# Chunk 0's inverse in two separate chains by halves of the heads, its first MLP layer split by token halves, and a new order of all steps

## The chip, the cores and the metric

The kernel runs on one core of a Trainium2 chip. The metric is the device time of one execution in microseconds (us), lower is better. Five engines work side by side: TensorE (PE, matrix products, with PEld for its weight loads), VectorE (DVE), ScalarE (ACT), GpSimd (POOL) and SyncE (SP, which here only issues loads and stores). ACT and POOL issue some loads too.

## The reference

Four batch rows of 768 tokens with eight heads of 48 columns pass through a delta rule (a matrix state per head, corrected token by token), and the result through one normalised MLP with 1536 hidden columns and a residual.

```python
k_n = k / (norm(k) + 1e-06)
for t in range(S):
    y[:, :, t] = einsum('bhd,bhde->bhe', q[:, :, t], state)
    v_old = einsum('bhde,bhd->bhe', state, kt)
    state = state + bt * einsum('bhd,bhe->bhde', kt, vt - v_old)
x = y.transpose(0, 2, 1, 3).reshape(B, S, H * D)          # (4, 768, 384)
xn = (x - mu) / sqrt(var + 1e-06) * g_ln
out = x + maximum(xn @ w_ch1, 0) @ w_ch2                   # 384 -> 1536 -> 384
```

## The kernel before

**Chunks.** The 768 tokens are worked in 12 chunks of 64. With two batch pairs and the heads there are 32 small problems per chunk; they lie in two halves, g = 0 and g = 1 (eight heads each of two batch rows). Inside a chunk the delta rule is a triangular system: with G = K K^T (`gram`) one needs an inverse X of a unit triangular matrix, then u = X v (`prod_u`), the output y (`out_y`), and the new state (`state_up`). After that come the layer norm (`xln`), its transpose with the factor g_ln (`xnt`), and the MLP of the chunk (`mlp`). Chunk 1's inverse, and those of the pairs 2-3, 4-5 and so on, are made row by row on DVE (`rows_inverse`, lines 916 and 923: two small operations a row).

**Chunk 0's inverse** (`first_inverse`, lines 716 to 802) is on the way of everything at the start, and so is made by doubling. After a first block (multiply L752, predicated copy L761, transposes L767, and three ACT copies `back`, L738) there are five levels n = 1..5. A level of a half g is: product E (PE, L780, 16 products of 64 by 64), a predicated copy out of PSUM (DVE, L785), product Z (PE, L795), and two ways out of Z's PSUM tile: two DVE transposes (`nat`, L744, needed by E of the next level) and three ACT copies (`back`, L738, needed by Z of the next level). Which PSUM pair a product writes comes from a list `order` (L1599): the pairs `two`, `by` and `f0/f1` in turn, i % 3. A product may only overwrite a pair when all readers of what was there are done. A pair `f0/f1` is two tiles, so that its predicated copy is two operations; the others need one.

**Chunk 0's u, y, norm.** u of half g goes to `two` (g = 0) or `by` (g = 1), L1078; y L1104; x L1142 on ACT; statistics on DVE; xln L1160; the transposes of both halves to `by` (L1192); xnt L1208 on ACT for g = 0 and L1198 on DVE for g = 1.

**MLP of chunk 0** (`mlp(0)`, L1409). The first layer is 12 blocks of 128 hidden columns, each three products (L1416) of 128 rows by 256 tokens, both halves at once, then one relu on ACT (L1425). fp32 products show up twice in the trace, so a block is six matmul rows. The second layer (L1438) is two sums of 12 products.

**Order.** Nothing is scheduled on the chip. The steps are recorded with `add`, each with its engine and what it reads and writes, and the list `ORDER` (L131) says in which order they are emitted; `in_this_order` keeps that order on each engine. An `f` in the list is a product of zeros (`zeros`, L1591, two matmul rows) that gives PE something to do. In the built program each load or store on the queues of SP and ACT also waits for the one eight places earlier in that written order (both queues counted together) to have landed. SP's loads of the diagonal blocks `gb` for chunk 1's inverse (from `gd`, the stored gram matrix) are in that chain, and ACT's square root `nrm_b` (L892) reads them.

**Weights.** The MLP weights come as 64-bit words and are converted on chip: two ACT operations (`hi` L593, `lo` L601), one DVE shift (L598) and one POOL sum (L611) for each piece. These fill the first 75 us beside chunk 0.

**End.** The last chunk's results go out by `put` (L1455): four stores on SP.

Of the kernel before, what the change touches and what calls it, by code (L numbers as in the profile page):

```python
# [16 lines left out]
C = 64  # L17
# [114 lines left out]
53 9 54 8 47 0 10 76 52 1 11-12 5 13 57 35 39 4 79 55 48 59 61 36 58 49 66 37 80 56 38 43 62 40 75 6-7 65 71 86 257  # L132
89 63 85 96 90 41 91 24 18 97 42 81 44 98 2 23 64 73 26 99 15 21 92 87 82 69 83-84 14 88 33 100 50 402 105 101-102
74 93 104 94 30 95 72 17 106 20 19 124 107 103 108 118 70 109 16 125 77 110 226 119 111 27 29 32 31 112 126 128 120
f f f 133 127 123 130 325 121-122 67 78 129 404 238 113 215 326 114 131 134 406 115-116 132 22 234 f 135 117 316 216
141 136 34 137 147 144 140 209 403 145 138 411 142 139 143 146 407 148-149 214 222 68 151 150 228 210 264 240 157
265 211 154 262 155 25 153 232 315 28 227 156 212 266 229 162 313 152 248 159 f 163 414 158 230 165 164 260 160-161
314 166 51 168 244 167 263 174 170 259 220 169 261 239 173 180 176 241 327 171 175 172 181 409 45 177 183 246 217
245 410 182 178 184 328 179 250 258 413 f f 185 60 191 189 256 317 242 401 186-187 196 46 193 190 197 192 188 247
318 194 199 267 195 213 198 268 319 363 200-201 243 269 205 320 270-271 273 203 f 321 272 208 274 202 275-276 204  # L140
277 249 207 278 322 251 279-280 3 364 281 f f 329 282 206 283 224 284 638 337 285-286 323 339 287 331 324 330 340
288 332 650 342 289-290 370 338 333 469 344 291-292 235-236 341 293-294 369 295-296 334 297 347 335 298-300 252 223
336 348 301 405 231 302 343 225 408 218 f f f f f 361 303 237 304 352 254 353 412 345 640 362 253 652 346 354 477
415 f 435 349 233 365 350 359 475 434 255 219 351 367 309 366 308 360 437 368 f f 355 310 376 375 312 436 221 358 f
f f 438 311 399 356-357 306 382 575 416 307 439 642 305 470 577 641 474 576 473 476 579 578 639 371 417 440 373 381
581 372 377 767 374 580 614 379 378 583 418 387 380 442 419 584 388 766 478 587 479 420 480-481 582 482 485 585 769
588 394 484 400 486 421 487 586 488-489 393 654 490-491 385 615 492 637 771 493 422 383 591 768 644 494 764 651 495
389 423 589 649 496 592 497-498 424 499 590 656 500 772 501 643 502 770 503 763 595 504 428 505 426 773 506 395 507
593 390 425 508 427 596 509 429 510 441 511 433 512 431 645 432 616 430 397 599 513 1052 443 514 594 396 655 391 515
653 444 516 483 517 398 774 600 445 518 1054 908 601 907 446 448 447 519 1056 910 520 909 521 657 522 646 449 384  # L150
523 386 629 451 597 524 647 1055 525 452 392 526 450 648 527 453 1051 454 528 658 1064 1058 617 659 602 1066 598 660
603 455 912 765 458 456 529 618 459 530 619 531 1053 532 620 533 1057 621 534-535 604 661 665 605 536 460 662 606
537-538 663 607 630 608 539 457 609 540-541 664 610 542-544 775 545 631 546 461 547 776 465 548 622 902 467 466 611
623 913 462-463 900 624 464 468 625 666-667 778 668-670 550 626 672 777 1068 673 911 549 805 674-675 551 676-678 809
632 806 679 552 680 807 681 1158 682-683 633 613 811 808 1157 684 810 685 914 686 813 687 904 688-689 1159 690 815
1059 814 627 812 901 817 691 1526 905 553 1160 692 554 693 818 694 816 819 695 556 779 555 557-558 823 696 1528 820
697-698 559 471 824 699 821 829 560 832 700 562 915 830 561 1070 563 822 780 701 1063 1163 702 831 564 838 906 781
703 825 704-705 1530 706 839 784 707 1067 1164 634 1165 708 782 612 785 835 709 786 565 710 1525 787 840 836 711 841
788-789 842 791 833 843 1167 792 472 712 827 783 628 834 1156 713 916 671 714 1166 828 844 715 1162 826 793 855 569
903 716 848 567 837 717 849 1155 568 790 718 850 1069 566 856 719 794 1168 857 720 858 845 721 1169 859 722 851 1529  # L160
795 723 852-853 796 847 860 724 917 797 846 570 862 801 725 571 918 726 1532 798 727 802 728 1531 854 800 865 729
799 1527 866 730 804 873 731 803 732 1065 874 573 733 875 734 574 919 735 920 736 572 921 1170 867 922 861 1352 876
635 877 1344 878 636 923 739 1071 868 740 956 924 869 957 737 870 1060 871 879 738 872 880 1537 1061 925 1161 1062
1072 948 891 1073 892 881 949 882 927 1074 883 926 1345 884 930 885 864 931 962 1354 953 1538 741 863 1171 886 951
742 1079 1172 958 887 1077 980 928 888 1346 929 893 752 1075 932 894 1076 935 895 963 746 1350 1173 1078 959 744 743
896 1540 964 897 950 936 1175 960 1533 965 954 745 1174 961 983 937 933 955 939 747 966 984 934 749 952 981 751 750
982 938 748 968 1080 940 967 1081 1356 1082 985 1348 1176 1083 969 1084 1087 1347 974 889 1177 1086 1351 1088-1090
1355 972 1091 975 1092 890 1093-1094 942 1095 989 1096 970 898 1097-1098 1634 1099-1100 1178 1353 971 1203 1101 973
944 1102 1180 1103 1824 2014 1104-1105 1630 753 1542 1106 1179 990 1358 1204 756 991 941 978 1085 1357 1107 899 986
992 979 1349 976 1108 987 943 1109 996 993 1633 977 999 1110 754 1000 997 1111 757 994 1001 755 1112 2016 1002 995  # L170
1359 1016 988 1017-1018 947 998 1003 1637 945 1006 2013 1007 946 1008 1205 1004 1019 1005 1020-1021 1113 1009 1639
1022 1024 1114 1010 1636 1023 1011 1031 1014 1115 1360 1012 1116 1209 1117 758 1641 1118 1025 1119 1640 760 1541
1026 1120 759 1629 1032 1361 1013 761 1027-1028 1218 1029 1211 1033 1030 1642 1362 1222 1182 1643 1207 1181 1185
1638 1042 1183 1631 1034 1015 1186 1035 1190 1043 762 1121 1036 1208 1122 1212 1184 1123 1213 1187 1124 1044 1544
1214 1045 1125 1046 1364 1543 1047 1363 1226 1126 2018 1037 1188 1048 1365 1038 1191 1049 1192 1189 1215 1366 1127
1219 1128 1216 1129 1367 1130 1230 1193 2017 1220 1131-1132 1223 1221 1368 1231 1224 1539 1227 1217 1534 1039 1225
1206 1194 1232 1535 1195 1228 1133 1632 1245 1233 1229 1239 1050 1259 1234 1240 1264 1536 1235 1545 1246 1241 1236
1254 1247 1134 1248 2026 1135 1196 1250 1249 1136 1210 1546 1644 1041 1242 1137 1547 1829 1138 1251 1197 1139 1243
1252 1040 1260 1244 1261 1198 1265 1140 1262 1199 1255-1256 1237 1548 1263 1266 1828 1141 1253 1257 1369 1142 1258
1143 1267 1645 1144 1268 1145 1269 1146 1201 1147 1273 1646 1270 1238 1274 1282 1276 1283 1271 1275 1284-1285 1280  # L180
1148 1286 1272 1149 1551 1292 2028 1287 1150 1658 1277 1288 1552 1202 1278 1550 1200 1290 1299 1293 1279 1294 1300
1289 1301 1831 1302 1281 1295-1296 1303 1635 1309 1553 1310 1297 1152 1304 1549 1298 1311 1305 1312 1317 1291 1396
1833 1318 1307 1830 1319 1554 1313 1151 1392 1314 2030 1320 1153 1315 1321 1308 1324 1322 1154 1306 1325 1323 1393
1834 1555 1371 1399 1326 1556 1335 1316 1397 1825 1557 1370 1336 1558 1561 1337 1823 1394 1327 1821 1395 1328 1560
1407 1329 1832 1562 1338 1403 1330 1339 2015 1372 1408 1373 1331 1340 1398 1400 1411 1563 1401 1341 2031 1564 1343
1409 1374 1402 1412 1404 1647 1826 1410 2032 1405 1565 1835 1413 1566 1406 1426 1414 1567 1648 1568 1440 1415 1427
1423 1649 1569 1420 1376 1445 1651 1377 2029 1421 1375 1570 1650 1416 1435 1422 1424 1332 1652 1417 1379 1334 1653
1380 1571-1572 1428 1381 1654 1660 1431 1657 1655 1429 1656 1378 1432 1430 1659 1382 1418 1433 1661 1425 1446 1573
1662 1574 1441 1836 1447 1419 1436 1434 1437 1448 1663 1575 1449 1383 1438 1450 1384 1333 1442 1576 1439 1577 1451
# [68 lines left out]
def kernel(  # L258
# [131 lines left out]
    def half(e):  # L390
        return slice(C * e, C * e + C)
# [638 lines left out]
    def recur(c, pr, lag=0.0):  # L1030
# [158 lines left out]
        for g in range(2) if c <= LNPE else ():  # L1189
            def turn(g=g):  # L1190
                for t in range(KC):
                    nc.tensor.transpose(by[:, g, t * 128 : (t + 1) * 128], xlns[g][:, t * 128 : (t + 1) * 128], ident)  # L1192
# [259 lines left out]
    def o_keys(g):  # L1452
        return [("o", g, n) for n in range(2)]
# [285 lines left out]
```

## Time and profile before

| what | value |
|---|---|
| runs | 534.24, 537.71, 536.07 us; median 536.07 |
| the profiled execution | 533.75 us, of which the profile's span is 532.0 |
| PE busy | 497.6 us (94%) |
| DVE, POOL, ACT busy | 366.4, 281.3, 207.9 us |
| first E product / last Z product of chunk 0's inverse | 21.70 / 46.58 us |
| chunk 0's first MLP product | 68.32 us |
| product of chunk 1's queries (`two` <- `qt,kt`, L828) | 67.23 us |
| last product ends / the four last stores are issued / span ends | 527.24 / 526.93 to 529.49 / 532.0 us |

A profile row such as "L785 DVE COPY_PREDICATED gsb<-u,two 128x512" is line 785 of the kernel, on DVE, writing `gsb` from `u` and `two`. Behind a bar stand the busy time and the mean time of one; behind a second bar the idle time of that engine just before, with what ended it. "issue" means that the engine waited for nothing that the profile shows.

### The profile page before, as it was taken

To read this page: it belongs to the slowest core of one execution; us is meant where nothing else is said; L and a number is where in the kernel's file an instruction comes from. 1 tells how busy PE (TensorE), PEld (TensorE's weight loads), DVE (VectorE), ACT (ScalarE), POOL (GpSimd) and SP (SyncE) were. 2 spreads that over 40 slices of the span, in tenths; PEclk is the share of its full clock that TensorE was granted. 3 is DMA by queue.
4 is the path that set the end of the run, shared out by engine and by line. 5 is a ranking of instruction groups with operands and counts; after the bars stand their busy time and mean duration, and the time that the engine had idled before them with its cause. 6 is when DMAs were issued, how large, how long until landed. Compare 5 with 4: busy or idle time off the path is not lost.

```text
span 532.0 us, 22724 instructions
## 1 busy us (share of the span) xinstructions
PE 497.6 (94%) x9942; PEld 451.9 (85%) x9942; DVE 366.4 (69%) x819; ACT 207.9 (39%) x451; POOL 281.3 (53%) x447
## 2 busy tenths in 40 slices
PE   5978798989989999999999999999999999999996
PEld 2766676758778888899999899999999999999996
DVE  3677748899996697994799982789985546244241
ACT  5677645412423332343342433442422623524130
POOL 6015574460573948757827617464266353554554
PEclk9789999999989999999999999999999999999999
DMA  9948798357635657156625157532435411212011
GB/s 174 289 73 194 178 207 160 78 111 139 119 58 120 150 115 123 34 141 154 100 65 97 21 135 198 116 70 33 101 74 104 91 31 37 56 40 53 1 30 31
DMA packets 181635, 54.56 MB, mean 103 GB/s; under 512 B 164888, under 2 KB 177312, under 8 KB 181536
## 3 DMA queue, kind: packets, MB, share of 16 engines
q1 hardware_dynamic: 168672, 40.30, 37.2%
q10 hardware_dynamic: 10656, 9.64, 6.6%
q0 software_dynamic: 2208, 3.17, 3.8%
q8 instruction: 78, 1.28, 1.0%
q14 instruction: 21, 0.17, 0.1%
HBM read 36.30 MB, written 16.78 MB: 100 GB/s over the span
## 4 chain that ended last, share of the span: by engine, by line
PE 67%; DVE 18%; issue 4%; ACT 2%; DMA 1%; POOL 1%; SPq 0%; ACTq 0%; DVEq 0%; POOLq 0%
PE f L1513 26%; PE f L1316 22%; DVE tmp L916 5%; PE f L1416 5%; DVE xb L923 4%; PE two L828 3%; PE by L1042 2%; PE two L1042 2%; PE by L1104 1%; PE two L1097 1%; DVE qt L923 1%; PE two L1114 1%; ACT xt L738 1%; DVE words L1488 1%; DVE st L1148 1%
## 5 line engine op out<-in xcount | busy, mean ns | idle before, releaser
L1513 PE MATMUL f<-w_sb,h_all 128*128 128x192 f32 x396 | 83.8, 331 | 1.8 <-issue 1.6
L1500 POOL TENSOR_TENSOR h_all<-h_all 128x256 f32<-128x256 f32 x99 | 73.9, 759 | 13.8 <-DVE tmp L916 6.3
L1513 PE MATMUL f<-words,h_all 128*128 128x192 f32 x396 | 80.0, 333 | 0.6 <-POOL h_all L1500 0.6
L1538 POOL TENSOR_TENSOR words<-h_all 128x128 f32<-128x128 f32 x66 | 30.3, 477 | 78.2 <-ACT h_all L1343 51.6
L1513 PEld LDWEIGHTS f<-words,h_all 128*128 128x128 f32 x396 | 66.0, 192 | 2.3 <-POOL h_all L1500 1.4
L1339 DVE TENSOR_TENSOR h_all<-f,h_all 128x512 f32<-128x512 f32 x72 | 48.8, 685 | 27.0 <-PE f L1316 22.0
L1513 PEld LDWEIGHTS f<-w_sb,h_all 128*128 128x128 f32 x396 | 65.7, 191 | 1.5 <-ACT words L1544 0.3
L916 DVE TENSOR_TENSOR tmp<-xb,gb 128x31 f32<-128x31 f32 (+19 forms) x139 | 60.2, 433 | 4.4 <-POOL xb L903 1.5
L923 DVE TENSOR_TENSOR xb<-xb,tmp 128x31 f32<-128x31 f32 (+19 forms) x139 | 55.5, 399 | 2.9
L410 POOL DMA_DIRECT2D tb<-in_k_dram x64 | 41.7, 655 | 20.5 <-DVE xb L923 9.3
L1416 PE MATMUL f<-xnt,w_sb 128*128 128x256 f32 x216 | 51.2, 384 | 0.0
L1334 ACT COPY h_all<-f 128x512 f32<-128x512 f32 x45 | 25.9, 586 | 61.6 <-PE f L1316 42.0
L1343 ACT ACTIVATE h_all<-h_all 128x512 f32<-128x512 f32 x54 | 32.9, 627 | 35.9 <-DVE h_all L1339 35.8
L1416 PEld LDWEIGHTS f<-xnt,w_sb 128*128 128x128 f32 x216 | 39.9, 190 | 7.3 <-issue 1.8
L1316 PE MATMUL f<-xnt,w_sb 128*128 128x128 f32 x288 | 41.1, 278 | 0.0
L1316 PE MATMUL f<-x_new,w_sb 128*128 128x128 f32 x288 | 40.7, 277 | 0.0
L1316 PEld LDWEIGHTS f<-x_new,w_sb 128*128 128x128 f32 x288 | 37.1, 191 | 0.4
L1316 PEld LDWEIGHTS f<-xnt,w_sb 128*128 128x128 f32 x288 | 36.7, 191 | 0.6
L611 POOL TENSOR_TENSOR w_sb<-words 128x768 uint32<-128x768 uint32 (+1 forms) x11 | 15.6, 1425 | 35.9 <-ACT xt L738 23.2
L1531 DVE TENSOR_TENSOR o<-f,x 128x192 f32<-128x192 f32 x33 | 11.3, 353 | 31.6 <-PE f L1513 29.1
L1142 ACT COPY x<-by 128x384 f32<-128x384 f32 x23 | 10.4, 480 | 43.8 <-DVE o L1531 28.1
L1425 ACT ACTIVATE h_all<-f 128x256 f32<-128x256 f32 x36 | 13.3, 380 | 36.0 <-PE f L1416 35.9
(252 smaller groups left out, 989.6 us busy)
## 6 DMA issues: line engine op xcount, KB each, us to landing
words<-in_moe_w_ch_dram ACTq DMA_DIRECT2D x20, 384.0 KB, 5.3
gd<-gsb SPq DMA_DIRECT2D x11, 512.0 KB, 3.1
v<-in_v_dram SPq DMA_DIRECT2D x24, 192.0 KB, 4.3
out_dram<-o SPq DMA_DIRECT2D x48, 96.0 KB, 2.3
kr<-in_k_dram SPq DMA_DIRECT2D x46, 96.0 KB, 3.7
xld<-xlt SPq DMA_DIRECT2D x9, 384.0 KB, 2.9
xnt<-xld SPq DMA_DIRECT2D x36, 96.0 KB, 2.8
tb<-in_q_dram SPq DMA_DIRECT2D x40, 64.0 KB, 3.2
```

What stands on the lines that cost most here:

```text
L410: add(eng, cost, lambda: QUEUE[eng].dma_start(out=out_, in_=in_), r, w, bulk=n * ns / 16e3, np=n, **kw)
L916: lambda j=j, n=n, w=w, t=t: nc.vector.tensor_tensor(out=t, in0=xv[:, 0:n, j : j + 1].to_broadcast([128, n, w]), in1=gv[:, j : j + 1, j + ...
L923: "DVE", dve(n * w), lambda t=t, rest=rest: nc.vector.tensor_tensor(out=rest, in0=rest, in1=t, op=ALU.subtract),
L1042: nc.tensor.matmul(dst[half(e), hp, j], src[drows(hp), (e if n else key_half(c, hp, e)) * GP + j], s_all[drows(hp), e, j], start=(n == 0 o ...
L1316: nc.tensor.matmul(wide(p[:, f : f + 128]), w[:, f : f + 128], r, start=start and i == 0, stop=True, skip_group_check=True)
L1334: add("ACT", act(512), lambda: nc.scalar.copy(o, p), pk, ok)
L1339: add("DVE", dve(512), lambda: nc.vector.tensor_tensor(out=o, in0=x, in1=y, op=op), [*xk_, *yk], ok)
L1343: add("ACT", act(512), lambda: nc.scalar.activation(o, o, ACTF.Relu, scale=scale), [], ok)
L1416: nc.tensor.matmul(p[:, 0:TOK], w1_sb[:, t, f * 128 : (f + 1) * 128], xnt[:, t], start=(t == 0), stop=(t == KC - 1))
L1500: add(eng, cost, lambda: e.tensor_tensor(out=out_, in0=x, in1=y, op=op), r, w, port=2 if eng == "Pool" else 1, pr=-2)
L1513: lambda f=f, t=start and f == order[0]: nc.tensor.matmul(p[:, 0:D2], lhs(f), rhs[:, f], start=t, stop=(f == order[-1]), skip_group_check=True
L1538: lambda f=f + i: e.tensor_tensor(out=s3[f], in0=one(0, 0)[0](f), in1=one(1, 0)[0](f), op=ALU.subtract),
```

## The change

1. `order` (L1599) becomes `PAIRS[i % 2]`: half 0 always uses `two`, half 1 always `by`. The predicated copies that were two operations (on `f0/f1`) become one: three DVE operations fewer.
2. The transpose of xln of half 0 goes to `two` instead of `by`.
3. Chunk 0's first layer is 24 blocks of three products over 128 tokens, first the 12 of half 0, which need xnt of half 0 alone, then the 12 of half 1; 24 relus of 128 instead of 12 of 256.
4. The two stores of the last chunk that belong to e = 1 are issued by ACT instead of SP.
5. `ORDER` is new as a whole, with 26 zero products instead of 21.

```diff
-    order = [PAIRS[i % 3] for i in range(22)]
+    order = [PAIRS[i % 2] for i in range(22)]
...
+            ps, bk = (by, BY[2 * g : 2 * g + 2]) if c or g else (two, TWO[:2])
...
-        for f in range(FT):
+        for g, f in ((g, f) for g in range(0 if c else 2) for f in range(FT)):
+            p, pk = bank()
+            cols = slice(g * 128, g * 128 + 128)
...
+                        p[:, 0:128], w1_sb[:, t, f * 128 : (f + 1) * 128], xnt[:, t, cols], start=(t == 0), stop=(t == KC - 1)
...
+            add(
+                "ACT", act(128), lambda f=f, p=p, cols=cols: nc.scalar.activation(h_all[:, f, cols], p[:, 0:128], ACTF.Relu),
+                pk, [("h", f, g)], pr=-5,
+            )
...
-                "SP", out[2 * e + g, c * C : (c + 1) * C, :], os_[g][half(e)], C, 105, o_keys(g), [("out", c, g, e)], pr=-5
+                "ACT" if e and c == NCH - 1 else "SP", out[2 * e + g, c * C : (c + 1) * C, :], os_[g][half(e)], C, 105, o_keys(g), [("out", c, g, e)], pr=-5
```

What the new `ORDER` does at the start, read from both lists (En.g is E of level n and half g; z is a zero product; kt, ktB, q, k2, k3, q1 are transposes of keys or queries; g is the first gram product of a half, G1 to G3 those of chunks 1 to 3; P is a half of chunk 0's queries product and P1 that of chunk 1):

```
PE before: z512 z512 kt.1 kt.0 z512 beta ktB g.1 ktB g.0 G1 zzz E1.1 E1.0 q q z Z1.0 Z1.1 E2.0 P E2.1 Z2.0 P Z2.1 z E3.0 E3.1 Z3.0
           Z3.1 E4.0 E4.1 zz Z4.0 Z4.1 k2 E5.0 k2 E5.1 Z5.0 Z5.1 z G2 zz k3 u.0 u.1 k3 y.1 G3 y.0 zzzzz state z q1 xln.1 q1 zz xln.0 zzz P1 M M M ...
PE after:  z512 z512 beta z512 kt.1 kt.0 g.0 ktB ktB g.1 G1 z q zzzzz q E1.1 E1.0 z Z1.0 Z1.1 zzzz E2.0 z Z2.0 zzzz E2.1 E3.0 Z2.1 Z3.0
           zz P E3.1 E4.0 P Z3.1 Z4.0 k2 zzz E5.0 k2 Z5.0 E4.1 G2 Z4.1 zzzz E5.1 u.0 Z5.1 k3 y.0 k3 z u.1 xln.0 G3 y.1 M M M state
           M q1 M xln.1 M q1 M P1 M M M ...      (M: a block of chunk 0's first layer)
ACT after, between the second multiply of the start and E3.0 (c: an L738 copy; w: a weight conversion; d: a load issued; n: a short copy;
           s: a copy of the stored gram): s c d w n c c s c d w w d c n n c n w cccc w w w w w w ccccc
DVE after, from Z3.0 to E5.0: t t root reciprocal w t w w w mult t w mult Pred.E3.1 Pred.E4.0 mask mult t mask t t t
```

ACT and POOL also start otherwise: ACT issues its two loads of chunk 0's keys first and the weight loads later (before, weight loads came between), and POOL issues the two loads of beta (`brow`) first of all, ahead of its index rows. The square root `nrm_b` of chunk 1's inverse is placed between Z3.0 and E4.0 (before: after E5.1). G2 and G3 (the gram products of chunks 2 and 3) stand behind E4.1 and u.1.

## The prediction, made before the changed kernel ran

> **What bounds the kernel now.** I read first the share of each engine, then the stretches of the run, then the chain that ended last for the start alone, then PE's rows there.
>
> ```profile
> PE 497.6 (94%) x9942; PEld 451.9 (85%) x9942; DVE 366.4 (69%) x819; ACT 207.9 (39%) x451; POOL 281.3 (53%) x447
> ```
>
> PE is busy for 94% of the span, but 69% on DVE and 39% on ACT are averages. Busy time by stretch (columns: stretch, length, PE, PEld, DVE, ACT, POOL, granted clock, DMA share):
>
> ```profile
> 0.00:22.00 22.00, 15.91 (x184) 10.11 (x187) 10.79 (x45) 11.63 (x22) 8.41 (x22) 0.84 1.08 213
> 22.00:34.00 12.00, 9.26 (x330) 8.01 (x321) 6.55 (x17) 9.09 (x24) 0.29 (x1) 0.86 0.72 172
> 34.00:45.00 11.00, 9.01 (x328) 7.18 (x331) 8.55 (x22) 9.49 (x23) 7.22 (x9) 1.00 0.63 100
> ...
> 80.00:165.00 85.00, 76.71 (x1821) 61.77 (x1820) 78.58 (x178) 31.43 (x76) 40.09 (x57) 0.98 0.58 111
> ...
> 250.00:500.00 250.00, 248.19 (x4487) 239.40 (x4487) 164.96 (x351) 90.29 (x191) 131.88 (x232) 1.00 0.36 77
> ```
>
> From 250 us on PE is full and nothing but PE work counts. From 80 to 165 us DVE is nearly full (78.58 of 85). Before 68 us a chain runs, and there ACT is the fullest engine (9.09 of 12, 9.49 of 11). What that chain is made of, between 12 and 70 us:
>
> ```profile
> by line: issue 10.0%; ACT xt L738 8.6%; PE f L1591 6.3%; PE f L1416 2.9%; DVE qt L744 2.9%; ACT words L601 2.8%; PE f L828 2.2%; PE f L637 2.1%; PE two L1114 1.9%; PE two L828 1.9%; PE f L795 1.5%; ACTq L410 1.5%; ACT words L593 1.4%; PE tw
> ```
>
> The ACT copies out of Z (L738) and weight conversions (L601, L593) stand on it, zero products (L1591) too, and "issue": PE standing still for nothing the profile shows. One such stop, in PE's rows:
>
> ```profile
> 26.55 0.41 PE L828 MATMUL f<-qt,kt 48*64 48x64 f32 x15
> 28.62 0.79 PE L828 MATMUL f<-qt,kt 48*64 48x64 f32 x17 [1.66 <-issue]
> 29.11 1.16 PE L780 MATMUL by<-qt,gsb 64*64 64x64 f32 x32
> ```
>
> So a gain can come from the first 68 us only: chunk 0's MLP starts at 68.32, and the 21 zero products (0.43 to 0.44 apart, 9 us) and PE's idle time before it are what can be had.
>
> **The change part by part.** The measure is where the queries product P1 stands (67.23) and how much first-layer work is done by then: none before; in the new order seven of the 24 half blocks stand ahead of it. I follow the new order by hand with the durations of the rows.
>
> *A level alone.* From a product's start to DVE's read 0.83 (E4.1 39.16, copy 39.99), predicated copy 0.73, to Z 0.1, Z's start to ACT's first copy 0.93 (41.16, 42.09), three copies 1.13, to E 0.1: 3.8 us. Before, E1.1 to E5.0 took 21.70 to 43.33, 5.4 a level. E of a half now writes the pair that Z of the same half left, so it waits for three ACT copies and two transposes, where before E.0 found a pair free. What else stands in ACT's and DVE's queues decides.
>
> *To E1.* Beta is loaded first: 6.4 us from issue to use as before (7.11 to 13.52) gives 8.4 instead of 13.52. But POOL's index rows, on which DVE's zero tile hangs, come behind those two issues: the first zero product at 4.0, not 2.23, and a third of 1.9 us stands ahead of the key transposes, which took 1.94 for eight. They end at 12.5, not 9.2. Behind them ACT copies (0.58), loads its table (1.28), takes two roots (0.25 each) and copies again; DVE then has 17 small operations (before: 11 in 1.74, so 2.7), two multiplies, two predicated copies, two transposes (4.2): E1 at 22.4. **+0.7.**
>
> *E1 to E3.0.* ACT has, from the predicated copy (20.7) to the last of six copies, these at 0.40, three conversions 0.55, three loads 0.4, small copies and a gram copy, 6.4 us: 27.1 (before 22.7). Z1 at 26.4 and 27.2. A short copy, a conversion and four copies more, 29.35: E2.0 29.5, Z2.0 31.15. Six conversions (3.7) and four copies (1.5) later E2.1 can write its pair: 34.6, and E3.0 follows at 35.1 (before 33.82). **+1.3.**
>
> *E3.0 to E5.0.* Z3.0 37.05. DVE's next row is the root of chunk 1's rows, which needs ACT's root, which needs eight loads `gb`. The fifth waits in its place for a weight load issued by ACT at 25.6 and landing 5.3 later (the median of those 20 loads), 31; the last is issued about 35.1 and lands 3.3 later, 38.4, while ACT is there at 37.05. Root, reciprocal, four shifts (0.42) and two transposes: E4.0 41.9 (37.59). A shift, two predicated copies, two masks (0.69), one multiply, four transposes: E5.0 47.5 (43.33). **+4.2.**
>
> *To P1.* A shift, row operations (0.21) and a predicated copy: Z5.0 49.3. ACT's copies of it, behind gram and key copies, end at 54.6; u.0 54.9, u scaled on DVE, y.0 57.1, x 58, xln 60.6, xnt 62.8. The first half block starts at 63 (68.32). Then three blocks, state 65, its copy 0.8, P1 at 71.0. That is 3.8 later, with 7 x 6 products of 0.111 (10.27 us for 92, L1316) = 4.7 us done: **-0.9 on PE.** What is late next is x1's row chain on DVE: its loads follow G3, which is later (61, before 54.3), but they are no longer behind all eight `xq`; I put nothing on it, ends -3 and +4 (from its start at 79.84, which waited for `gb` 1.1, and from P1's 3.8).
>
> *Stops.* The walk has no "issue" stops; the old time holds 1.66, 0.56, 0.74 and 1.46 between 26 and 57, 4.4 us. PE waits more often now, so some fall into waits: half, **+2.2**, ends 0 and 4.4. The Trainium skill ("Runtime: NRT & Kernel Launch", Instruction fetch mechanics) says that instructions come in blocks of 256 and that this is mostly hidden; by that the stops cost nothing and the sum would be 2.2 lower, 535.5. The trace has such blocks (q8: 78 packets, 1.28 MB) but also the 1.66 us above.
>
> *First layer split.* 144 products of 128 columns at 0.111 to 0.120 against 72 of 256 at 0.227 (4.08 for 18): -0.3 to +1.0, **+0.4**. Relus 24 x 0.30 against 12 x 0.38 on ACT, +2.6 us, beside PE work, as ACT is busy 5.79 of 11.70 us there; without that cover the three PSUM tiles would hold PE.
>
> *ACT's load in the relus.* A weight load stands behind the sixth relu and waits for the load eight places earlier (`xq`, issued about 67.5 and landing 4.5 later, 72), when ACT is there at 71: 0 to 1, **+0.5**; relus and the x1 root are queued behind it.
>
> *Transposes of xln to `two`, fewer predicated copies.* Inside the walk. More zero products: they sit where PE waits; 4 before E5.1 end at 53.8, the copies it waits for at 54.2, so nothing.
>
> *Last stores.* Four issues took 2.56 us in one queue; two queues side by side save one of the last pair, **-0.6**, ends 0 and -1.3.
>
> *The rest of the order.* By the state product of chunk 3 (165 us) the same PE work and the same DVE work is in both lists, and the same to 4% at the states of chunks 5 to 10: 0, ends -3 and +3 (a quarter of PE's idle time from 68 to 250, 12 us).
>
> Sum: -0.9 + 2.2 + 0.4 + 0.5 - 0.6 = **+1.6** on the profiled execution: 533.75 gives 535.35. That execution lies 2.3 below the median of the three runs (536.07), so the median goes to **537.7**.
>
> **The rivals.**
>
> *A: the two chains run near their floor (faster).* Five levels at 3.8 would bring E5.0 to 22.4 + 15.2 = 37.6; with three shifts and the root's wait gone from the way (1.3 + 1.4 + 0.7) and the six conversions elsewhere (3.7) it is 40.4, 7.1 before my 47.5: 530.6. For it: 8.6% of the old chain is L738. Against it: the conversions stand in the written order ahead of the copies, and nothing overtakes. It decides if E5.0 is before 43.
>
> *B: half clock in the chain (slower).* Granted clock 0.84 and 0.86 up to 34 us, 1.00 after; at half clock a product of a half took 1.16 (29.11), not 0.69. Two products a level, five levels, 0.47 each: +4.7, 542.4. For it: more waits on ACT; against: 20 of the 26 zero products stand between E1 and u.1. The Trainium skill ("TensorE: Matmul & The Clock Gate", Part 1) says half clock is the default, and returns after an idle window of 3.4 us. The trace agrees in kind: half clock rows follow the idle stretches before 13.52 and 28.62.
>
> *C: DVE's row chain starts later (slower).* From 80 to 165 DVE has 6.4 us of slack in 85. If x1's `gb` lands as much later as P1, +3.8 goes through to 165: 541.5. For it: G3 at 61. Against: the new list has less DVE work ahead of it (x1's multiply after 49.8 us of DVE work instead of 53.0).
>
> *D: the change does not part the chains.* On ACT and DVE both halves share one queue in fixed order, so the halves are parted in PSUM alone; that is in my forecast (E2.1 and E3.0 wait for the same row of copies).
>
> **How the numbers follow.** A measurement of this kernel can tell about 1% (5.4 us) from no change: below 530.7 faster, above 541.4 slower. Forecast 0.42, A 0.32, B 0.13, C 0.13. About 0.27 of A lies under 530.7, the rest with the forecast, whose own range with +-4 for the walk is 533 to 542; from it 0.04 goes to slower, with most of B and C: faster 0.27, same 0.44, slower 0.29. For 8 in 10: down to A with 3 us from the rest of the order, 528, and up to B with C's 3.8, 546.
>
> **What would show it.** Right: E2 of half 1 waiting for an L738 copy; DVE idle ahead of `nrm_b` at about 37 until a `gb` load lands; E5.0 at 45 to 50; first half block at 60 to 66 and P1 at 68 to 74; the last two stores side by side. Wrong: E5.0 before 43 (A); clock under 0.8 from 22 to 45 (B); x1's multiply after 82 us (C); or PE idle between 80 and 250 changed by more than 4 us, for which I have no step.

## The result, and the profile after

The changed kernel is slower: 552.98 us (median of four runs, 551.59 to 554.66) against 536.89 us for the kernel before on the same chip; the ratio is 1.030 with a 95% interval of 1.024 to 1.036. The prediction said 537.7 us, 528 to 546. The profiled execution took 551.77 us, its span 549.7. Of the ten executions of run e13 below one took 1720.24 us; it is in the median given there and not in the ratio.

First the page of the profile after: busy time by engine, and the chain that ended last.

```profile
PE 505.3 (92%) x10024; PEld 458.5 (83%) x10024; DVE 375.3 (68%) x816; ACT 209.5 (38%) x463; POOL 280.3 (51%) x447
...
PE 56%; DVE 23%; DMA 7%; SPq 5%; issue 5%; ACT 2%; POOL 2%; ACTq 0%; DVEq 0%; POOLq 0%
```

PE's share of that chain fell (67% before), DVE's rose (18% before), and so did those of DMA and SP's queue (1% and 0% before). The same stretches as before (stretch, length, PE, PEld, DVE, ACT, POOL, granted clock, DMA share, GB/s):

```profile
22.00:34.00 12.00, 11.07 (x214) 8.69 (x215) 4.85 (x11) 9.21 (x24) 5.96 (x10) 0.74 0.71 164
34.00:45.00 11.00, 10.05 (x338) 8.08 (x336) 9.74 (x24) 8.58 (x20) 3.07 (x4) 1.00 0.70 113
80.00:165.00 85.00, 75.14 (x1783) 59.12 (x1781) 76.67 (x159) 32.32 (x79) 42.87 (x57) 0.98 0.58 116
165.00:250.00 85.00, 76.85 (x1818) 68.96 (x1819) 73.37 (x139) 25.20 (x60) 52.41 (x70) 0.96 0.49 96
250.00:500.00 250.00, 244.86 (x4633) 235.94 (x4633) 163.84 (x353) 91.25 (x193) 128.34 (x226) 1.00 0.40 86
```

The stretch that the prediction did not show, in the kernel before:

```profile
165.00:250.00 85.00, 81.70 (x1886) 74.63 (x1885) 64.53 (x128) 28.30 (x62) 58.90 (x79) 1.00 0.56 119
```

From 165 to 250 us PE lost 4.85 us of busy time, while DVE became 8.84 us busier with 11 instructions more. The start is not where most of it went. I add up the usual durations of the products issued up to a milestone and call the rest of the time lost (fillers, idle time and half clock together; single executions, so good to a few us):

| PE's milestone | before: time / lost | after: time / lost | lost more |
|---|---|---|---|
| queries product of chunk 1 (P1) | 67.2 / 32.8 | 73.6 / 34.4 | 1.6 |
| state of chunk 3 | 165.4 / 47.9 | 174.6 / 55.9 | 8.0 |
| state of chunk 4 | 195.6 / 50.4 | 212.3 / 58.1 | 7.7 |
| state of chunk 6 | 273.5 / 56.3 | 295.9 / 74.1 | 17.8 |
| last product's end | 527.2 / 65.2 | 545.8 / 83.3 | 18.1 |

What PE waited for from 165 to 300 us, before and then after (engine and line, waited for: total us, times, longest):

```profile
PE f L1513 <- issue: 1.6, 1, 1.6
PE two L1114 <- issue: 0.8, 1, 0.8
PE two L1042 <- issue: 0.6, 1, 0.6
PE two L1042 <- DVE pt L859: 0.5, 1, 0.5
```

```profile
PE f L1526 <- DVE o L1544: 3.5, 2, 2.3
PE f L1310 <- DVE o L1544: 3.4, 2, 2.5
PE f L1310 <- DVE h_all L1333: 1.9, 1, 1.9
PE f L1310 <- POOL xnt L1293: 1.4, 1, 1.4
```

Before, PE never waited there for DVE's sums out of PSUM. After, it waits for them five times: `o` (L1544, L1531 before) adds the second layer's result to x and frees its PSUM tile; `h_all` (L1333) does so for the first layer. One of these waits, from its cause. First the row operation of the same width in the kernel before, then DVE's rows after (start, duration):

```profile
195.43 0.32 DVE L923 TENSOR_TENSOR xb<-xb,tmp 128x156 f32<-128x156 f32 x1
```

```profile
204.98 5.12 DVE L916 TENSOR_TENSOR xb<-xb,tmp 128x156 f32<-128x156 f32 x1
210.13 0.34 DVE L909 TENSOR_TENSOR tmp<-xb,gb 128x175 f32<-128x175 f32 x1
...
215.56 0.35 DVE L1544 TENSOR_TENSOR o<-f,x 128x192 f32<-128x192 f32 x1
```

POOL's rows in that time:

```profile
204.72 0.65 POOL L403 DMA_DIRECT2D tb<-in_k_dram  x1
205.38 0.74 POOL L1513 TENSOR_TENSOR h_all<-h_all 128x256 f32<-128x256 f32 x1
206.07 1.27 POOL L1270 TENSOR_TENSOR w_sb<-w_sb 128x512 f32<-128x512 f32 x1
207.29 0.71 POOL L1513 TENSOR_TENSOR h_all<-h_all 128x256 f32<-128x256 f32 x1
207.97 1.25 POOL L1270 TENSOR_TENSOR w_sb<-w_sb 128x512 f32<-128x512 f32 x1
209.20 0.72 POOL L1513 TENSOR_TENSOR h_all<-h_all 128x256 f32<-128x256 f32 x1
```

And PE's:

```profile
213.18 0.59 PE L1526 MATMUL f<-w_sb,h_all 128*128 128x192 f32 x2
216.06 2.26 PE L1526 MATMUL f<-words,h_all 128*128 128x192 f32 x6 [2.28 <-DVE o L1544]
```

An operation of 0.3 us (the next one, larger, takes 0.34) stood for 5.12 us, until POOL's five sums in a row were through. Behind it stand 13 more row operations of the inverse of chunks 6 and 7, then `o`; PE waits for `o` 2.28 us. The Trainium skill ("SBUF — State Buffer", Who interferes with whom) says that a DVE operation with two SBUF inputs contends with a POOL operation that reads SBUF, that the ports they share are an exclusive lock, and that issue order decides which of the two blocks. By that a held row is what is to be expected, but for two things: it stood behind five POOL instructions, not one, and its row begins 0.40 us ahead of the first of them (204.98 and 205.38), while POOL was issuing a load. What held it over that time the runs do not show.

Such a long stand is rare. I call a row operation of the inverses held when it took 0.2 us more than the shortest of its line and shape. Before, 47 of the 310 are held, each by one POOL sum. After, 42 are held, 39 of them by one sum, and three by four or five: those at 204.98 us (5.12), 218.30 (4.21) and 279.03 (2.57). Three of PE's five waits for DVE's sums out of PSUM end behind them, at 216.06 (2.28), 226.57 (2.49) and 282.41 (1.89).

### The profile page after: what moved, and what is told of

It reads as the page before. It is cut to its first block, busy times and chain, and to the rows that moved or that the text cites. A ratio compares the mean times of both kernels' runs of the same rounds, so it can differ in the third digit from the quotient of the medians.

```text
span 549.7 us, 22922 instructions
## 1 busy us (share of the span) xinstructions
PE 505.3 (92%) x10024; PEld 458.5 (83%) x10024; DVE 375.3 (68%) x816; ACT 209.5 (38%) x463; POOL 280.3 (51%) x447
## 4 chain that ended last, share of the span: by engine, by line
PE 56%; DVE 23%; DMA 7%; SPq 5%; issue 5%; ACT 2%; POOL 2%; ACTq 0%; DVEq 0%; POOLq 0%
PE f L1526 19%; PE f L1310 18%; DVE xb L916 6%; DVE tmp L909 6%; SPq L403 5%; PE f L1429 4%; PE two L821 2%; DMA words<-in_moe_w_ch_dram 2%; DMA gd<-gsb 2%; DVE qt L916 1%; PE f L1451 1%; DVE xln L1153 1%; PE by L1035 1%; PE by L1097 1%; DMA xt<-xd 1%
## 5 line engine op out<-in xcount | busy, mean ns | idle before, releaser
L916 DVE TENSOR_TENSOR xb<-xb,tmp 128x31 f32<-128x31 f32 (+19 forms) x139 | 69.4, 499 | 3.0
L1333 DVE TENSOR_TENSOR h_all<-f,h_all 128x512 f32<-128x512 f32 x72 | 48.7, 684 | 29.0 <-PE f L1310 27.4
L909 DVE TENSOR_TENSOR tmp<-xb,gb 128x31 f32<-128x31 f32 (+19 forms) x139 | 54.7, 393 | 3.2
L1310 PE MATMUL f<-xnt,w_sb 128*128 128x128 f32 x288 | 39.7, 277 | 2.2 <-POOL xnt L1293 1.4
L1544 DVE TENSOR_TENSOR o<-f,x 128x192 f32<-128x192 f32 x33 | 11.2, 353 | 40.3 <-PE f L1526 33.6
L1310 PEld LDWEIGHTS f<-xnt,w_sb 128*128 128x128 f32 x288 | 36.2, 192 | 3.0 <-POOL xnt L1293 1.6
L1429 PE MATMUL f<-xnt,w_sb 128*128 128x256 f32 x144 | 33.8, 384 | 0.0
L1429 PEld LDWEIGHTS f<-xnt,w_sb 128*128 128x128 f32 x144 | 26.7, 190 | 4.1 <-issue 0.2
L1526 PE MATMUL f<-w_sb,words 128*128 128x192 f32 x132 | 27.1, 328 | 0.0
```

The costliest lines, as they stand in the source:

```text
L909: lambda j=j, n=n, w=w, t=t: nc.vector.tensor_tensor(out=t, in0=xv[:, 0:n, j : j + 1].to_broadcast([128, n, w]), in1=gv[:, j : j + 1, j + ...
L916: "DVE", dve(n * w), lambda t=t, rest=rest: nc.vector.tensor_tensor(out=rest, in0=rest, in1=t, op=ALU.subtract),
L1310: nc.tensor.matmul(wide(p[:, f : f + 128]), w[:, f : f + 128], r, start=start and i == 0, stop=True, skip_group_check=True)
L1333: add("DVE", dve(512), lambda: nc.vector.tensor_tensor(out=o, in0=x, in1=y, op=op), [*xk_, *yk], ok)
L1429: nc.tensor.matmul(p[:, 0:TOK], w1_sb[:, t, f * 128 : (f + 1) * 128], xnt[:, t], start=(t == 0), stop=(t == KC - 1))
L1526: lambda f=f, t=start and f == order[0]: nc.tensor.matmul(p[:, 0:D2], lhs(f), rhs[:, f], start=t, stop=(f == order[-1]), skip_group_check=True
```

## The experiments

Two theories stood at first beside a late start (S): P, that POOL's lost waits do it, and O, that the place of the steps on each engine does. The written list decides on those waits: `emit` lets a POOL step wait for the last DVE step with two SBUF inputs that stands ahead of it in the list ("shared port"), once for each such DVE step. In the old list 126 of POOL's 374 steps wait so, in the new one 54. Later theories: L (DVE and POOL exclude each other at the MLP's POOL sums), T (POOL's own length), Q (SP's queue). Each ratio below is to the kernel before on the same chip.

| run | us | ratio, 95% interval |
|---|---|---|
| e1 finer places for POOL's steps | 556.85 | 1.040 (1.037 to 1.042) |
| e2 old kernel, no waits | 542.37 | 1.012 (1.008 to 1.015) |
| e3 new up to P1, then old | 540.52 | 1.010 (1.005 to 1.015) |
| e4 old up to P1, then new | 550.00 | 1.026 (1.020 to 1.032) |
| e5 / e6 sums on an eighth, old / new | 530.01 / 529.79 | 0.991 (0.987 to 0.995) / 0.993 (0.989 to 0.997) |
| e7 new up to chunk 3's state, then old | 538.92 | 1.007 (1.005 to 1.010) |
| e8 old up to chunk 3's state, then new | 547.82 | 1.023 (1.021 to 1.025) |
| e9 / e10 sums on an eighth, long memsets | 560.41 / 570.66 | 1.047 (1.042 to 1.053) / 1.066 (1.060 to 1.071) |
| e11 old up to chunk 6's state, then new | 540.70 | 1.011 (1.005 to 1.018) |
| e12 as e8, SP in the old order | 587.40 | 1.097 (1.093 to 1.101) |
| e13 / e14 sums on an eighth, matched memsets | 533.55 / 533.64 | 0.997 (0.994 to 1.000) / 0.999 (0.996 to 1.002) |
| e15 / e16 short row operations, old / new | 524.62 / 541.08 | 0.981 (0.977 to 0.985) / 1.014 (1.010 to 1.018) |
| e17 as e16, finer places | 543.91 | 1.016 (1.011 to 1.020) |
| e18 as e16, no waits | 551.16 | 1.031 (1.028 to 1.035) |

### Where in the run (e3, e4, e7, e8, e11)

The two lists are joined at a moment of the trace: all steps begun by then in the order of one kernel, what is left in the order of the other (in e3 and e4 chunk 0's MLP steps are spread over the other list's places for them). In the edit, A(t) is what had begun by t in the trace of after, B(t) of before:

```diff
 e3:  ORDER = A(73.6) + (old list without A(73.6))
 e4:  ORDER = B(67.2) + (new list without B(67.2))
 e7:  ORDER = A(174.6) + (old list without it)
 e8:  ORDER = B(165.4) + (new list without it)
 e11: ORDER = B(273.5) + (new list without it)
```

> The changed kernel up to the queries product of chunk 1 (all that started before 73.6 us in its trace, in its order), then everything left in the order of the kernel before (121 POOL waits). It tells the first 74 us from the rest. P and O: the start alone costs what the trace shows by then, 1.7 us of PE's lost time and at most 3 more: 537 to 542. S: the later start is handed on and most of the loss is there: 546 to 553.

> The other half: the kernel before up to the queries product of chunk 1 (67.2 us), then what is left in the order of the changed kernel (59 POOL waits), first layer of chunk 0 not split. P and O: most of the loss is here, 546 to 552. S: near the kernel before, 536 to 540.

> The changed kernel up to the state product of chunk 3 (174.6 us in its trace), the rest in the order of the kernel before. PE had lost 8.0 us more than before by then. If each stretch of the new order loses its own time: 543 to 547. If the loss after that point is only the late start handed on by DVE's chains (S): nothing is won by the old rest, 549 to 555.

> The kernel before up to the state product of chunk 3 (165.4 us), the rest in the order of the changed kernel. Each stretch its own: +8 to +11, 544 to 548. S: near the kernel before, 535 to 539.

> The kernel before up to the state product of chunk 6 (273.5 us), the rest in the order of the changed kernel. With the old order up to 165 us only it took 13 us more. If that loss lies in the stretch between, where chunk 4's and 5's inverse on DVE runs beside the sums of chunks 2 to 4: 535 to 539 us. If it is spread over the rest: 541 to 546.

Measured: the new start alone costs 4.0 us (e3, interval 2.7 to 8.3), the new rest alone 13.5 (e4), so the loss is not a late start handed on. Up to chunk 3's state the new list costs 4.0 us (e7), after it 12.9 (e8), after chunk 6's state 5.3 (e11, interval 2.6 to 9.4). The halves add up (17.5 and 16.9 against 16.1), so those joins cost little. e7 came out below both ranges that were expected: the 8.0 us of the table are one execution's, and in e7's, with the same order up to there, chunk 3's state stood at 171.9 us and not at 174.6.

e11 lies between its two ranges, and its trace tells why. PE waits there once for long, right behind the join at 273.5 us:

```profile
280.38 2.29 PE L1509 MATMUL f<-w_sb,h_all 128*128 128x192 f32 x6 [4.30 <-ACT h_all L1339]
```

The granted clock is 0.69 from 274 to 285 us, and from 315 us on PE waits for nothing. The changed kernel has no such wait between 165 and 530 us, while e8 has those of the changed kernel (`o` 3.2 and 2.9 us, `h_all` 1.9, `xnt` 1.4). So e11's 5.3 us belong to its join, and no loss behind chunk 6's state is shown, as the table has it (17.8 and 18.1). Of the 16 us some 4 lie ahead of chunk 3's state, and the rest, some 12, between it and chunk 6's.

### The waits (e1, e2)

e1 moves only POOL's steps within the list; every engine keeps its own order. The place of the stuck operation, d1120, with POOL's (P) and DVE's (d) step numbers:

```diff
-P1008 P2035 P1007 P1226 P1017 P1224 P1018 P1563 d1109 ... P1006 d1115 d1380 d1116 d1117 d1106 d1118 d1119 d1120 d1121 ...
+... d1116 d1117 d1106 P1008 P2035 d1118 d1119 d1120 P1007 d1121 P1226 d1122 P1017 d1123 P1224 d1124 P1018 P1563 ...
```

e2 takes the waits out of the kernel before:

```diff
-if s.eng == "Pool" and "bulk" not in s.plan and shared is not seen:
+if False and s.eng == "Pool" and "bulk" not in s.plan and shared is not seen:
```

> The changed kernel; every engine keeps its own order, and the loads and stores of SP and ACT keep their common order. Only where POOL's steps stand among DVE's in the written list is new: 155 of POOL's 374 steps now wait for the DVE step ahead of them (54 in the changed kernel, 126 in the kernel before). Theory P (pacing): the changed list writes POOL's steps in long runs, so only the first of a run waits for DVE, the rest run back to back and hold DVE's row operations up (one took 5.12 us at 205 us); with the waits back, 8 to 12 of the 17 us return: 541 to 545 us. Theory S (late start of chunk 1: queries product at 73.6 instead of 67.2 us) and theory O (the order of PE's and DVE's own lists after 74 us): within 3 us of the changed kernel, 550 to 556.

> The kernel before, without the waits that hold a POOL step until the last DVE step ahead of it in the list (all 126 gone; no data depends on them). P: POOL runs free of DVE, its operations run together and DVE's row operations between 80 and 250 us are held up: slower by 5 to 12 us, 542 to 549. S and O: within 2 us of the kernel before, or a little faster for want of waits on POOL.

e2 is 5.9 us slower, at the low end of P's range: the waits are worth something. But e1 has 155 of them and is no faster than the changed kernel, 3.9 us slower by the medians. So the number of waits is not the cause. That is all that e1 rules out: its waits stand at other places than the old kernel's 126, and in the mixtures above the waits and the loss go together (121 and 107 waits in e3 and e7, 59 and 73 in e4 and e8). DVE's rows of e1 at the same place show what finer places do:

```profile
209.04 1.32 DVE L917 TENSOR_TENSOR tmp<-xb,gb 128x207 f32<-128x207 f32 x1
...
213.16 0.81 DVE L924 TENSOR_TENSOR xb<-xb,tmp 128x231 f32<-128x231 f32 x1
...
215.29 1.43 DVE L917 TENSOR_TENSOR tmp<-xb,gb 128x247 f32<-128x247 f32 x1
216.64 0.34 DVE L1552 TENSOR_TENSOR o<-f,x 128x192 f32<-128x192 f32 x1
```

The 5 us stand is gone, but most row operations here let one sum pass (1.32, 0.81, 1.43 for 0.4), and `o` starts at 216.64, not earlier than the 215.56 of the changed kernel. PE then waits 3.38 us. The profile puts that wait down to POOL's `x_new`, which ends at 217.03, 0.05 us after `o`; but of the two only `o` is among the steps that the product has to wait for.

### The sums (e5, e6, e9, e10, e13, e14)

The MLP's POOL sums (L1276, L1299, L1500, L1538 of before) go through a helper that works on an eighth of the columns; e9 and e10 put two memsets of the whole output ahead of each, e13 and e14 as many as make the step as long as the whole sum. Seven eighths of the sums are left out; tiles that would stay unwritten are zeroed once. The edit is shown in short:

```diff
+def eighth(e, o, x, y, op):
+    part = lambda ap: ap[(slice(None),) * (len(ap.shape) - 1) + (slice(0, ap.shape[-1] // 8),)]
+    e.memset(o, 0.0)      # e9, e10: twice; e13, e14: once, once and a quarter, or twice, by size; e5, e6: none
+    e.tensor_tensor(out=part(o), in0=part(x), in1=part(y), op=op)
...
-add(eng, cost, lambda: e.tensor_tensor(out=out_, in0=x, in1=y, op=op), r, w,
+add(eng, cost, lambda: eighth(e, out_, x, y, op), r, w,
```

> The kernel before with the MLP's POOL sums (L1276, L1299, L1500, L1538) on one eighth of their columns: seven eighths of these sums are left out, every step keeps its place. A price of POOL's sums in the old order, to be set against the same cut in the changed kernel. Theory L (POOL sums and DVE's two-input row operations exclude each other, and the new order makes them meet more): faster by 3 to 8 us, 529 to 534; DVE's stretched time after 165 us (some 23 us of the 39 between 68 and 300 us and later) mostly gone. Theory O (the place of the steps on each engine, with collisions of no weight): 0 to 3 us faster.

> The same cut in the changed kernel. L: the difference to the cut old kernel falls from 16 us to 8 or less, as the 10 us by which DVE's operations are stretched more after 165 us go: 536 to 541. O: the difference stays at 13 to 17 us: 544 to 550.

> The kernel before with the MLP's POOL sums on one eighth of their columns, and before each of them two POOL memsets of the whole output tile, which read nothing: POOL is busy about as long as with the whole sums, but reads SBUF only for an eighth (seven eighths of the sums are left out). Theory L (the two engines exclude each other where POOL reads SBUF beside DVE's two-input operations): like the cut without memsets, 528 to 533 us, DVE not stretched. Theory T (POOL's own length, PE waiting for late sums): back to the kernel before, 534 to 538.

> The same in the changed kernel. L: 528 to 534 us, no difference to the filled old kernel beyond 3 us. T: POOL as long as before brings the loss back, 545 to 553.

> The kernel before with the MLP's POOL sums on an eighth of their columns (seven eighths left out), each after memsets chosen so that the step is about as long as the whole sum (0.74, 0.46, 0.46 and 1.35 us for 0.746, 0.49, 0.47 and 1.3). L: DVE not stretched, 528 to 533. T: 534 to 539, as the kernel before.

> The same in the changed kernel. L: within 4 us of the matched old kernel. T: 12 to 17 us above it.

With the sums cut, the two kernels take the same time (530.01 and 529.79): the 16 us are gone, more than L expected. Part of that is PE's clock in single executions (last section), but the medians agree. The 4 us of the start are gone too, though none of these sums runs before 137 us: at chunk 0's state e6 is 5.3 us behind e5 (68.1 and 62.8 us), at chunk 3's it is level (167.4 and 167.0). e6 and e14 keep SP's new order and lose nothing, so SP's queue alone (Q) does not carry the loss either.

e9 and e10 came out above all ranges. Three instructions for one made POOL 42 us busier than in the kernels (323.5 against 281.3 us), and both are slower, by 25.0 and 35.3 us, with little stretch on DVE (17.7 us each, by the measure below): PE waits in e9 12.4 us for POOL's `h_all` alone, against 0.6 before. So POOL's length does cost time where it grows. With matched memsets POOL is busy for 272.5 and 270.4 us, 3% less than in the kernels, and the two again take the same time (533.55 and 533.64), where T had put e14 12 to 17 us above e13. For the old kernel that is no clear gain (533.55 lies between the ranges of L and T), for the changed one, by the ratios, some 17 us. What is mostly gone there is POOL's reading of SBUF: the instruction that reads takes 0.27 us instead of 0.75 for `h_all`. DVE's operations, summed over what each took above the median time of its line and shape, are stretched by 17.0 and 15.6 us, against 37.3 before and 45.3 after, and none of the long stands is left. PE's waits of e14 from 165 to 300 us are down to two:

```profile
PE f L1537 <- POOL h_all L58: 0.7, 1, 0.7
PE f L1321 <- POOL xnt L58: 0.2, 1, 0.2
```

So the loss goes through the sums, and at this length POOL's time alone does not carry it. One doubt stays: a memset needs no input, so the part of the step behind its last input is shorter than in a whole sum (less so for the 99 sums `h_all<-h_all`, which write over one of their inputs: there the memset too waits for that input).

### The row operations (e15 to e18)

The row operations of the inverses of chunks 2 to 11 work on a quarter of their columns; the rest is left out.

```diff
+            less = max(1, w // 4) if L == BK else w
...
-                    out=t, in0=xv[:, 0:n, j : j + 1].to_broadcast([128, n, w]),
...
+                    out=t[:, :, 0:less], in0=xv[:, 0:n, j : j + 1].to_broadcast([128, n, less]),
...
-                "DVE", dve(n * w), lambda t=t, rest=rest: nc.vector.tensor_tensor(out=rest, in0=rest, in1=t, op=ALU.subtract),
+                "DVE", dve(n * w), lambda t=t[:, :, 0:less], rest=rest[:, :, 0:less]: nc.vector.tensor_tensor(out=rest, in0=rest, in1=t, op=ALU.subtract),
```

e17 has e1's list beside it, e18 the changed kernel's list with e2's edit.

> The kernel before with POOL's sums whole, but DVE's row operations of the inverses of chunks 2 to 11 (L916, L923; two a row) on a quarter of their columns; three quarters of that work are left out. L: DVE gets the time that it was held up and more, 526 to 531. T: POOL's length is unchanged, 533 to 536.

> The same in the changed kernel. L: within 4 us of the old kernel with short rows, as DVE and POOL no longer fill each other's time. T: POOL's sums are as long and as late as before, 10 to 17 us above it.

> The changed kernel with the finer places of POOL's steps (155 waits, as in e1) and DVE's row operations on a quarter of their columns (three quarters of that work left out, as in e16). L: POOL waits only for short DVE operations and DVE only for one POOL operation, so most of the 16.5 us between e15 and e16 go: 526 to 533 us. Theory O (the place of the steps on the engines as such): as e16, 538 to 544.

> The same short rows in the changed kernel without any of the waits that hold POOL for DVE. L: runs of POOL's sums are held up by nothing, so DVE is stuck as long or longer than in e16: 540 to 548 us. O: as e16, 538 to 544.

Here L, as I had put it, failed: short rows make both kernels faster (e15 more than either theory had it), but 16.5 us still lie between them (e15, e16), as T said, and finer places win nothing (e17, as O said). e18 came out above both ranges, 10 us slower than e16, in L's direction. The rows of e16 show what was wrong with the expectation:

```profile
200.81 5.11 DVE L910 TENSOR_TENSOR tmp<-xb,gb 128x42 f32<-128x42 f32 x1
205.95 0.21 DVE L917 TENSOR_TENSOR xb<-xb,tmp 128x42 f32<-128x42 f32 x1
```

An operation of 0.21 us stands as long as the long one did (again its row begins ahead of the first of the five sums, by 0.52 us). What a meeting costs is set by POOL's work, not by the length of DVE's operation: one sum as a rule, a whole run of them in a few cases. With finer places (e17) most short operations still let a sum pass, and `o` still stands behind them all; DVE's rows, then three of POOL's sums back to back, through which DVE does get in:

```profile
209.88 0.66 DVE L918 TENSOR_TENSOR tmp<-xb,gb 128x60 f32<-128x60 f32 x1
...
211.25 1.84 DVE L918 TENSOR_TENSOR tmp<-xb,gb 128x52 f32<-128x52 f32 x1
213.02 0.34 DVE L1553 TENSOR_TENSOR o<-f,x 128x192 f32<-128x192 f32 x1
```

```profile
209.05 2.10 POOL L1522 TENSOR_TENSOR h_all<-h_all 128x256 f32<-128x256 f32 x3
```

So e15 to e17 do not speak against the exclusion, but against its price as I had set it. What lets a whole run pass in one case and a single sum in another is not shown. That the number of row operations ahead of `o` decides is read from these rows; it was not tried by itself.

### SP's order (e12)

```diff
 e12: B(165.4), then PE, DVE, ACT and POOL in the new order, SP in the old
```

> The kernel before up to 165 us, then the new order on PE, DVE, ACT and POOL, but the old order of SP's loads and stores. L: the loads are not what is late, 545 to 549 us as with SP's new order. Theory Q (SP's queue: stores of the gram matrix and of xd stand ahead of loads that DVE waits for, as at 252 to 267 us): 536 to 542.

It took 587.40 us, outside both ranges. PE waited there 13.7 us at once for `o`; I take it that the loads come in an order that the other engines' new lists do not fit. It tells nothing on Q. Behind chunk 3's state this is also the only way to give some engines the new order and others the old; every other such mixture closes a circle of steps waiting for each other. Which engine's list carries the loss could therefore not be tried.

No mixture was faster than the kernel before.

## Why the prediction was wrong, step by step

**The start was right in its times, in part by luck.** E1 was to come at 22.4 and came at 23.53; E2.1 34.6 and 34.71; E3.0 35.1 and 35.35; Z3.0 37.05 and 36.97; E4.0 41.9 and 41.05; E5.0 47.5 and 45.91. E4.0 and E5.0 did wait for ACT's copies (0.25 and 0.62 us). E2 of half 1 shows no such wait, though it was to be the sign: it came as the four zero products ahead of it were through, 0.60 us after the last copy out of its pair (34.11). The root was not late, as I had it (38.4): ACT took it at 36.15. Between Z5.0 (49.3 and 47.66) and u.0 (54.9 and 57.14) a stop came, longer than any in the kernel before:

```profile
52.07 1.14 PE L821 MATMUL f<-kt 48*64 48x64 f32 x32 [2.78 <-issue]
...
65.45 1.74 PE L1409 MATMUL f<-xnt,w_sb 128*128 128x128 f32 x13
```

The first half block came at 65.45 (63), P1 at 73.58 (71.0), with seven half blocks done as predicted. With 1.6 us more lost by P1 the sum up to there (-0.9 and +2.2 of stops) was near, but errors cancel in it: E5.0 was 1.6 us early, u.0 2.2 late.

**The first layer split was mis-sized.** I took +0.4, ends -0.3 and +1.0. From the start of each block to the next product's start they took 22.9 us in sum, against 16.6 before. Of these 6.3 us the products and the changes between them are some 1.8 (a product at its usual pace takes 0.112 us, 16.1 for 144, against 15.6 for 72 before). PE's idle time is the other 4.5. Of it 1.8 us are waits of later products for DVE's `xnj`, which the split does not explain. The rest is idle time ahead of the blocks themselves, as PE's waits from 68 to 165 us have it:

```profile
PE f L1409 <- issue: 2.2, 2, 2.0
PE f L1409 <- ACT h_all L1417: 0.6, 2, 0.4
```

Stops I had counted for the chain only, and relus I had laid beside PE's work. All of the start and this together is the 4.0 us of e3 and e7; +1.6 was predicted.

**Rivals.** A did not come (E5.0 at 45.91, its mark was 43). B came in part: the granted clock was 0.74 from 22 to 34 us, E1's two products took 1.13 and 1.08; but from 34 to 45 us it was 1.00. C's mark (x1's multiply after 82 us) was not reached: it came at 80.03, 79.84 before. The row chain behind it ended 6.7 us later all the same (127.8 and 121.1). D holds for the queues of ACT and DVE.

**The last stores were right.** I took -0.6. From the start of the last DVE sum to the span's end 4.7 us passed before and 3.8 after; the issues, first before, then after:

```profile
526.93 2.56 SPq L410 DMA_DIRECT2D out_dram<-o  x4
```

```profile
545.51 1.27 SPq L403 DMA_DIRECT2D out_dram<-o  x2
545.52 1.38 ACTq L403 DMA_DIRECT2D out_dram<-o  x2
```

**The step that failed** is "*The rest of the order.* ... 0, ends -3 and +3 (a quarter of PE's idle time from 68 to 250, 12 us)". It measured +13.5 us (e4), nearly all of it from chunk 3's state on (+12.9, e8). I compared amounts of work up to milestones, found them equal, and set the bounds by the idle time that the old kernel had. Neither bounds anything: a list can make idle time that was not there. In its place the runs showed time lost through POOL's sums (with them cut, the two lists take the same time), and the rows show DVE held by them while what PE needs stands behind. The prediction named as its own refutation a change of PE's idle time between 80 and 250 us by more than 4 us; it is 6.4 (76.71 + 81.70 = 158.41 us of 170 busy before, 75.14 + 76.85 = 151.99 after).

What is shown: the stretch of the list where it is lost (e3, e4, e7, e8); that it goes through POOL's sums, and not through their length alone (e5, e6, e13, e14); that neither the number of POOL's waits (e1) nor the length of DVE's row operations (e16, e17) is the cause. What is read from rows alone: that `o` and `h_all` late behind held row operations are what PE pays for. Open: what lets a whole run of sums pass a DVE operation, what the old places of POOL's waits are worth in the new list, and which engine's list would have to change.

## What to carry to other kernels

When a list of steps is replaced as a whole, equal amounts of work up to each milestone do not settle the time; look for the operations that free PSUM, and count what stands ahead of them on their engine and which other engine can hold that up. Where operations of DVE and POOL, each with two inputs in SBUF, lie side by side, count POOL's time for DVE too: here a held operation cost one sum as a rule and a whole run of them at worst, however short it was itself. A bound taken from the idle time of the old kernel bounds a gain, not a loss.

## What the runs showed of the hardware that was not expected

**A DVE operation can stand behind a whole run of POOL's.** 5.12 us behind five sums (after), 5.11 for a 0.21 us operation (e16). It is the exception: 39 of the 42 held row operations of the changed kernel let one sum pass.

**PE's clock can fall after a short wait.** The stretches around the wait of 2.28 us shown above (same columns as before):

```profile
213.00:216.00 3.00, 0.77 (x26) 0.42 (x14) 2.79 (x9) 0.00 (x0) 0.34 (x1) 0.98 0.69 114
216.00:219.30 3.30, 3.25 (x10) 3.28 (x11) 3.27 (x4) 0.00 (x0) 3.29 (x5) 0.50 0.75 138
```

The clock halves as the work comes back and stays so for 3.4 us, which costs some 1.6 us more: this wait of 2.28 us costs about 4. By the trace's clock records the half-clock stretches of this execution, up to its last product, begin at 21.3, 52.0, 127.1, 215.9 and 226.1 us, whole multiples of 3.41 us apart, and last 3.41 or 6.83. The stop of 2.03 us that ends at 87.90 brought none. So a wait does not by itself cost a stretch; where it falls in that grid matters (read from this trace, not tried). Behind 68 us the changed kernel's execution has three such stretches, the old one's has one, e6's and e14's none, e5's and e13's two. Each is worth some 1.7 us, so single executions of like lists differ by a few us for this alone, and e5, e6, e13 and e14 are read by their medians. The Trainium skill ("TensorE: Matmul & The Clock Gate", Part 1) puts the fall after an idle window of about 3.4 us; here PE was busy for 1.27 of the 3.40 us from 212.5 to 215.9, ahead of the fall.
